# A fused attention and two-layer kernel: reciprocal root as one power operation on GpSimd, and another list scheduler's order

## The chip, the cores and the metric

The kernel runs on one core of a Trainium2 chip. The core has a matrix engine (TensorE, PE in the rows), whose weight loads are shown apart as PEld; VectorE (DVE), ScalarE (ACT) and GpSimd (POOL) for elementwise work; SyncE (SP), which here only issues transfers (DMA); and 16 DMA engines that move data between HBM and the on-chip memory. Each engine works off its own instructions in order; engines wait for each other through semaphores. The metric is the time of one execution in microseconds on the device; the median of three runs is quoted.

## What is computed

The reference has three parts, one after the other (cut to its core):

```python
# attention: q, k, v of 4 x 8 x 576 x 64
out_up    = np.repeat(sm_attn(mean4(q), mean4(k), mean4(v)), 4, axis=2)   # on means of 4 rows
out_local = softmax(where(|i - j| < 4, q @ k.T / 8, -1e9)) @ v            # a band of 7 keys
x = (out_up + out_local) as 2304 rows of 512
# first layer
h = x @ w_in                                       # 512 x 2048
x = (max(h, 0) + alpha * min(h, 0)) @ w_out        # 2048 x 512
# second layer
rms = np.sqrt(np.mean(x * x, axis=-1, keepdims=True) + 1e-06)
xn  = x / rms * rms_g
g   = xn @ w_gate                                  # 512 x 1536
return (g / (1 + exp(-g)) * (xn @ w_val)) @ w_out2 # 1536 x 512
```

The weights arrive as 64-bit floats.

## The kernel before

The 2304 rows are worked in six blocks of 384 (BW; half blocks of CW = 192), always with the rows along the free axis of a matmul and 128 features along the partitions. Each 32-bit product is made of three 16-bit matmuls, from a high and a low part of both operands (`split`, L373 and L374, makes the parts on ACT and DVE).

**Start.** Batch 0's attention needs q and k of each pair of heads transposed: `load` (L743) fetches each pair of heads in four transfers of 144 KB (two of q, two of k), PE transposes pieces of 96 rows (tps, L792), ACT copies three of them at a time to the tile T (L793, in all 16 such copies). Scores (lsps, L868 to L880, for the band; sps, L815, for the means), exponentials (L900, L825) and the sums over v follow. At the same time the weights of the first layer are made ready: a w_in tile of 768 KB is loaded (wr, L1091), decoded from 64-bit to 32-bit floats by two ACT instructions (L1110, L1113) and one on DVE (L1115), its size is measured on PE (sqps, L1131), and it is split.

**Stages.** `m1_first` runs the first layer for blocks 0 and half of 1, then `m1` and `m2` alternate over the blocks: `m1` (hps, L1371; acc, L1388) is the first layer, `m2` (gps, L1488; oacc, L1517) the second. In between stands `rms_tasks` for each of the six blocks: squares on ACT, column sums by matmuls with ones (ssps, L1309), in `ssum` the mean and its reciprocal root (the tile ry of 128x3 numbers, L1320 to L1330, eleven of its instructions on DVE the Newton iteration with its start value), in `bcast` three matmuls that spread ry over the partitions (rps, L1336), then the scaling (ra, L1345) and the split into x (L374). The attention of the other batches (prod, L478 and L526, partly on POOL; sd, L632) and the second layer's weights are cut into small tasks, which the slots of the stages call in the background.

**What sets the order.** The kernel is written out in program order first, and `issue_order` then reorders it: a list scheduler that gives each instruction a duration (`cost`), a delay to those that need its result (`waits`), and walks forward and backward over the graph in turn, 40 rounds, each with the end times of the last as priorities. The round with the earliest end of its own model is kept, and each engine's queue, the queue of SP included, is fixed in that order. Nothing of it is adjusted on the device: an instruction that waits holds all behind it on its engine. Eight transfers can be under way; the ninth issue waits until the first has landed.

Of the kernel before, what the change touches and what calls it, by code (L numbers as in the profile page):

```python
# [9 lines left out]
F32 = mybir.dt.float32  # L10
F16 = mybir.dt.float16
I32 = mybir.dt.int32
# [8 lines left out]
    return bass.AP(tensor=ap.tensor, offset=ap.offset + off, ap=[p] + [list(d) for d in dims])  # L21


def issue_order(tc, nc, groups, rounds=40):


    insts = [i for i in nc.cur_bb.bb.instructions if i.opcode != "TilePoolBoundary"]
# [22 lines left out]
    def psum(a):  # L50
        return "PSUM" in str(a.tensor.space)
# [34 lines left out]
    def cost(k, ins, outs):  # L86
        i, e = insts[k], eng[k]
        if not outs:
            return 60.0
        o, n = outs[0], free(outs[0])  # L90
        if e == "SP":
            return transfer(o, ins[0])[0]
        if e == "PE":
            if wide(ins[0]) == 2:
                return n / 2.4 + (2.5 if n > 128 else 50)
            return n * 2 / 2.4 + 4 if i.is_transpose else n * 4 / 2.4 + 100
        n = max([n] + [free(a) for a in ins[:1]])
        extra = len([a for a in ins[1:] if free(a) == 1 and n > 1])
        if e == "Activation":
            return (51 if psum(ins[0]) else 93) + n / 1.2 + 93 * (extra + len(outs) - 1)  # L100
        if e == "DVE":
            if i.opcode == "Reciprocal":
                return 89 + 6.25 * n
            fast = i.opcode in ("TensorScalarPtr", "TensorCopy") and not any(psum(a) for a in ins)
            fast = fast and len([a for a in ins if free(a) > 1]) < 2
            return 89 + n / (1.92 if fast else 0.96) + 60 * (extra > 0)
# [98 lines left out]
    def run(P, S, prio, fwd, d):  # L205
# [33 lines left out]
                        heapq.heappush(soon[eng[s]], (at[s], s))  # L239
        return end, seq, real  # L240

    prio, d, best = [float(-k) for k in count], dur, None
    for _ in range(rounds):
        end = run(succs, preds, prio, False, d)[0]
        end, seq, d = run(preds, succs, [-x for x in end], True, dur)
        prio = [-x for x in end]
        if best is None or max(end) < best[0]:
            best = max(end), seq
    info = mybir.DependencyInfo(mybir.DependencyClass.NoSync, mybir.DependencyReason.DATA)
    for q in best[1].values():  # L250
        for a, b in zip(q, q[1:]):
# [4 lines left out]
def kernel(  # L256
# [62 lines left out]
    ident = const.tile([128, 128], F32, name="ident")  # L319
    ones = const.tile([128, 1], F32, name="ones")  # L320
    nhalf = const.tile([128, 1], F32, name="nhalf")
    maskp = const.tile([128, 2, W, ND], F32, name="maskp")
    edge = const.tile([128, 3], F32, name="edge")
    pidx = edge[:, 2:3].bitcast(I32)
# [51 lines left out]
    def setup():  # L376
        nc.gpsimd.memset(ident, 1.0)
        nc.gpsimd.affine_select(
            out=ident, in_=ident, pattern=[[-1, 128]], compare_op=ALU.is_equal, fill=0.0, base=0, channel_multiplier=1
        )  # L380
        nc.vector.memset(ones, 1.0)
        nc.vector.memset(nhalf, -0.5 - 2.0 ** -20)
        nc.gpsimd.iota(pidx, pattern=[[0, 1]], base=0, channel_multiplier=1)
        nc.vector.tensor_scalar(out=edge[:, 0:1], in0=pidx, scalar1=HP, scalar2=NEG, op0=ALU.is_lt, op1=ALU.mult)
        nc.vector.tensor_scalar(out=edge[:, 1:2], in0=pidx, scalar1=(NC - 1) * HP, scalar2=NEG, op0=ALU.is_ge, op1=ALU.mult)
        nc.gpsimd.memset(maskp, 0.0)
        for t in range(W):
# [901 lines left out]
    def rms_tasks(m):  # L1289
# [23 lines left out]
        NT = BW // 128  # L1313

        def ssum():
            v_ = x1_p.tile([128, 3, NT], F32, tag="ry", name="ry")
            x, y, t_ = v_[:, 0], v_[:, 1], v_[:, 2]
            p = st["ps"][:, :, 0]
            if ne > 1:
                nc.vector.tensor_reduce(out=x, in_=st["ps"], axis=AX.X, op=ALU.add)  # L1320
                p = x
            nc.vector.tensor_scalar(out=x, in0=p, scalar1=1.0 / DM, scalar2=1e-6, op0=ALU.mult, op1=ALU.add)
            nc.vector.tensor_scalar(out=y.bitcast(I32), in0=x.bitcast(I32), scalar1=1, scalar2=None,
                                    op0=ALU.logical_shift_right)
# [421 lines left out]
```

## Time and profile before

| | |
|---|---|
| median of three runs | 969.99 us (968.99 to 970.92) |
| the profiled execution | 967.56 us |
| its span, from the first to the last instruction | 965.8 us |
| TensorE busy | 929.6 us, 96% |
| VectorE busy | 685.5 us, 71% |
| ScalarE busy | 481.7 us, 50% |
| GpSimd busy | 117.5 us, 12% |
| granted TensorE clock, mean | 0.991 of full speed |

The rows below come from one profiled execution. "Busy" is the share of time in which an engine has an instruction under way; a row of a group shows how often it stands (x), its busy time, the mean length of one, and the idle time just before it with what ended it. A row of the order of time may merge equal neighbours (x2). Lengths of matmuls contain their latency: the pace is read from a run of many.

### The profile page before, as it was taken

The numbers are of one execution on the slowest core, as the hardware profiler recorded it, in microseconds if no ns is written. First come the engines' busy times: TensorE is split into PE (matmuls) and PEld (weight loads), VectorE is DVE, ScalarE is ACT, GpSimd is POOL, SyncE is SP. The second block draws the span as 40 slices with busy tenths as digits, with TensorE's granted clock in tenths as the row PEclk, the third lists the DMA queues.
The fourth block names the chain that finished last, engine by engine and source line by source line (L and its number), as shares of the span: only waits on it lengthen the run. The fifth ranks groups of instructions, "written<-read, shape, count | busy, mean of one in ns | idle before, by whom it ended". The sixth has DMA issues, their size and how long they took to land.

```text
span 965.8 us, 16581 instructions
## 1 busy us (share of the span) xinstructions
PE 929.6 (96%) x6484; PEld 600.2 (62%) x6484; DVE 685.5 (71%) x1447; ACT 481.7 (50%) x1108; POOL 117.5 (12%) x96
## 2 busy tenths in 40 slices
PE   6978999999999999999999999999999999999998
PEld 4767777799655555565566655555556666555554
DVE  4789996998999978999987899963333442542333
ACT  5999889889864273233575322221322433321322
POOL 1101100201021103333102313210000000000000
PEclk9978999999999999999999999999999999999999
DMA  8886534574302142122122211000000000000000
GB/s 207 253 274 181 161 100 137 197 226 155 128 1 58 52 141 95 44 72 62 45 85 73 82 38 36 22 22 1 20 14 1 1 1 1 1 1 10 24 1 33
DMA packets 53712, 73.80 MB, mean 76 GB/s; under 512 B 22190, under 2 KB 35138, under 8 KB 53634
## 3 DMA queue, kind: packets, MB, share of 16 engines
q1 hardware_dynamic: 53634, 72.74, 24.9%
q8 instruction: 51, 0.84, 0.4%
q14 instruction: 27, 0.22, 0.1%
HBM read 68.01 MB, written 4.72 MB: 75 GB/s over the span
## 4 chain that ended last, share of the span: by engine, by line
PE 67%; DVE 13%; ACT 9%; issue 6%; DMA 5%; POOL 0%; SPq 0%; ACTq 0%; POOLq 0%
PE gps L1488 23%; PE hps L1371 12%; PE acc L1388 12%; PE oacc L1517 11%; DMA out_dram<-ob 4%; DVE prod L539 2%; DVE ls L489 1%; ACT wr L1110 1%; ACT dls L900 1%; DVE prod L526 1%; ACT wr L1113 1%; ACT wi L373 1%; DVE ghl L374 1%; DVE prod L478 1%; DVE hps L1377 1%
## 5 line engine op out<-in xcount | busy, mean ns | idle before, releaser
L1371 PE MATMUL hps<-xt,wi 128*128 128x192 f16 (+1 forms) x1536 | 357.0, 290 | 7.2 <-DVE g L374 3.8
L1488 PE MATMUL gps<-x,w 128*128 128x384 f16 x1728 | 339.0, 326 | 3.3 <-DVE th L1499 3.0
L1388 PE MATMUL acc<-ghl,wo 128*128 128x384 f16 (+1 forms) x960 | 253.8, 310 | 1.7 <-DVE ghl L374 0.6
L1488 PEld LDWEIGHTS <-w 128*128 128x128 f16 x1728 | 169.9, 99 | 118.4 <-issue 5.2
L1517 PE MATMUL oacc<-w,uhl 128*128 128x512 f16 x630 | 191.5, 379 | 2.3 <-ACT ob L1573 1.6
L1371 PEld LDWEIGHTS <-wi 128*128 128x128 f16 x1536 | 149.5, 100 | 59.4 <-issue 7.3
L1388 PEld LDWEIGHTS <-wo 128*128 128x128 f16 x1344 | 129.0, 98 | 61.7 <-issue 4.5
L1377 DVE SCALAR_TENSOR_TENSOR hps<-g,oma,hps 128x192 f32<-128x192 f32 (+1 forms) x128 | 66.0, 516 | 61.3 <-ACT g L1375 61.0
L1497 ACT ACTIVATE th<-gps,tsc 128x384 f32<-128x384 f32 x72 | 41.8, 580 | 132.3 <-PE gps L1488 131.8
L1517 PEld LDWEIGHTS <-uhl 128*128 128x128 f16 x630 | 61.6, 98 | 67.3 <-issue 2.4
L1499 DVE SCALAR_TENSOR_TENSOR th<-th,gps 128x384 f32<-128x384 f32 x72 | 39.6, 550 | 87.8 <-ACT th L1497 87.4
L1375 ACT ACTIVATE g<-hps 128x384 f32<-128x384 f32 x96 | 47.3, 493 | 84.1 <-PE hps L1371 83.5
L1508 ACT ACTIVATE uhl<-gps 128x384 f16<-128x384 f32 x72 | 41.7, 579 | 94.3 <-DVE gps L1502 85.5
L478 POOL TENSOR_TENSOR prod<-cq,ckv 128x896 f32<-128x896 f32 x24 | 54.8, 2284 | 191.6 <-DVE ls L489 50.6
L1388 PE MATMUL acc<-g,wo 128*128 128x384 f16 (+1 forms) x384 | 70.4, 286 | 0.0
L373 ACT ACTIVATE ghl<-hps,grp 128x384 f16<-128x384 f32 (+1 forms) x73 | 42.0, 576 | 51.2 <-DVE hps L1377 48.6
L1509 DVE TENSOR_TENSOR uhl<-gps,uhl 128x384 f16<-128x384 f32 x72 | 45.3, 629 | 28.1 <-ACT uhl L1508 27.8
L526 POOL TENSOR_TENSOR prod<-ls,ckv 128x896 f32<-128x896 f32 x24 | 43.6, 1816 | 163.3 <-DVE lo L539 70.6
L539 DVE TENSOR_TENSOR prod<-prod 128x384 f32<-128x384 f32 (+1 forms) x96 | 59.4, 630 | 4.3 <-POOL prod L526 4.3
L374 DVE SCALAR_TENSOR_TENSOR ghl<-hps,grp,ghl 128x384 f16<-128x384 f32 (+1 forms) x73 | 44.3, 607 | 23.9 <-ACT ghl L373 23.6
L489 DVE TENSOR_REDUCE ls<-prod 128x14 f32<-128x896 f32 x48 | 51.1, 1075 | 0.1
L1110 ACT ACTIVATE wr<-wr 128x768 f32<-128x768 f32 (+1 forms) x48 | 41.8, 877 | 6.2 <-DMA wr<-in_moe_w_out_dram 3.2
(242 smaller groups left out, 1138.9 us busy)
## 6 DMA issues: line engine op xcount, KB each, us to landing
wr<-in_moe_w_out_dram SPq DMA_DIRECT2D x18, 512.0 KB
wr<-in_moe_w_in_dram SPq DMA_DIRECT2D x10, 768.0 KB
wr<-in_moe_w_gate_dram SPq DMA_DIRECT2D x8, 768.0 KB
wr<-in_moe_w_val_dram SPq DMA_DIRECT2D x8, 768.0 KB
ckv<-in_k_dram SPq DMA_DIRECT2D x7, 768.0 KB
ckv<-in_v_dram SPq DMA_DIRECT2D x7, 768.0 KB
wr<-in_moe_w_out_dram SPq DMA_DIRECT2D x20, 256.0 KB
sd<-in_q_dram SPq DMA_DIRECT2D x24, 144.0 KB
```

Of the source, the lines that this page charges most:

```text
L373: nc.scalar.activation(out=hi, in_=src, func=AF.Copy, scale=s)
L374: nc.vector.scalar_tensor_tensor(out=lo, in0=src, scalar=s, in1=hi, op0=ALU.mult, op1=ALU.subtract)
L478: engs[i].tensor_tensor(out=pr, in0=view(st["q"][:, j, t:t + TP], [[D, TP], [0, ND], [1, D]]), in1=view(st["k"][:, j, t:t + TP], [[D, TP], ...
L489: nc.vector.tensor_reduce(out=st["s"][:, j, t:t + TP], in_=st.pop(("p", i)), axis=AX.X, op=ALU.add)
L526: engs[i].tensor_tensor(out=pr, in0=view(st["s"][:, j, t:t + TP], [[ND, TP], [1, ND], [0, D]]), in1=view(st["v"][:, j, t:t + TP], [[D, TP] ...
L539: add = lambda o, a, c: nc.vector.tensor_tensor(out=o, in0=a, in1=c, op=ALU.add)
L1110: nc.scalar.activation(out=hi.bitcast(F32), in_=hi.bitcast(F32), func=AF.Prelu, scale=2.0 ** -112, alpha=2.0 ** 32)
L1371: nc.tensor.matmul(ps[:, j], wi[:, f + j, a, kk * 128:(kk + 1) * 128], x[:, b_, kk, c0:c0 + n], start=(i == 0), stop=(i == 3 * KK - 1))
L1377: nc.vector.scalar_tensor_tensor(out=ps[:, j], in0=g[:, j], scalar=oma[:, f + j:f + j + 1], in1=ps[:, j], op0=ALU.mult, op1=ALU.add)
L1388: nc.tensor.matmul(acc[e], wo_f(f)[:, a, e * 128:(e + 1) * 128], hl[:, b_], start=(f == f0 and i == 0), stop=(f == f1 and i == 2))
L1488: nc.tensor.matmul(ps, w2_t[i0 + f // 3].rearrange("p a (k c) -> p a k c", k=KK)[:, a, kk, (f % 3) * 128:(f % 3 + 1) * 128], xh[:, b_, kk] ...
L1517: nc.tensor.matmul(acc[tt], t[:, a, tt * 128:(tt + 1) * 128], w[:, b_, f % 3], start=(f in first and i == 0), stop=(f in last and i == 2))
```

## The change

Three things change. `ssum` keeps the mean on DVE (L1320 and L1322) and replaces the eleven instructions of the Newton iteration by one on GpSimd: ry to the power -0.5, with a constant tile mhalf as exponent. In `issue_order` some durations of `cost` are other numbers (small matmuls, ScalarE with a stepped input, VectorE's fixed part and its reads from PSUM, 1200 ns for a GpSimd operation on up to four numbers). And the choice among the rounds changes: 100 rounds are run instead of 40, each candidate order within 8 us of the best so far is walked through by the new function `replay`, in which each queue is kept as it stands, under three sets of durations (as estimated; ScalarE 3% and transfers 10% slower; VectorE 3% slower and transfers 5% faster; each with another phase of the TensorE clock), and the smallest mean of the three ends is kept. Lines of the kernel proper stand 39 higher than before (L743 is L782, L1110 is L1149, L1322 is L1361), from `bcast` on 32 higher (L1336 is L1368).

```diff
-def issue_order(tc, nc, groups, rounds=40):
+def issue_order(tc, nc, groups, rounds=100):
...
             if wide(ins[0]) == 2:
-                return n / 2.4 + (2.5 if n > 128 else 50)
-            return n * 2 / 2.4 + 4 if i.is_transpose else n * 4 / 2.4 + 100
+                return max(25.0, n / 2.4 + 2.5)
+            return n * 2 / 2.4 + 3 if i.is_transpose else n * 4 / 2.4 + (128 if n < 64 else 8)
...
+        if n <= 4 and ins:
+            return 1200.0
...
-        if best is None or max(end) < best[0]:
-            best = max(end), seq
+        if best is None or max(end) < best[0] + 8000.0:
+            x = sum(replay(seq, *a) for a in trials) / len(trials)
+            if best is None or x < best[0]:
+                best = x, seq
...
+        nc.gpsimd.memset(mhalf, -0.5)
...
             nc.vector.tensor_scalar(out=x, in0=p, scalar1=1.0 / DM, scalar2=1e-6, op0=ALU.mult, op1=ALU.add)
-            nc.vector.tensor_scalar(out=y.bitcast(I32), in0=x.bitcast(I32), scalar1=1, scalar2=None,
-                                    op0=ALU.logical_shift_right)
-            nc.vector.tensor_scalar(out=y.bitcast(I32), in0=y.bitcast(I32), scalar1=-1.0, scalar2=float(0x5F3759DF),
-                                    op0=ALU.mult, op1=ALU.add)
-            for _ in range(3):
-                nc.vector.tensor_tensor(out=t_, in0=y, in1=y, op=ALU.mult)
-                nc.vector.scalar_tensor_tensor(out=t_, in0=t_, scalar=-0.5, in1=x, op0=ALU.mult, op1=ALU.mult)
-                nc.vector.scalar_tensor_tensor(out=y, in0=t_, scalar=1.5, in1=y, op0=ALU.add, op1=ALU.mult)
+            nc.gpsimd.tensor_tensor(out=y, in0=x, in1=mhalf.to_broadcast([128, NT]), op=ALU.pow)
```

The order changes nearly everywhere on the way, by a few places. Three places follow. The first is SP's queue at the start, from the fourth transfer on (wo holds the raw q and k, wr a raw weight tile). Before:

```order
L743 DMA wo<-in_k_dram 96x6x64
L743 DMA wo<-in_q_dram 96x6x64
L743 DMA wo<-in_k_dram 96x6x64
L743 DMA wo<-in_q_dram 96x6x64 x2
L743 DMA wo<-in_k_dram 96x6x64
L1650 DMA rows<-in_moe_alpha_dram 16x128
L1650 DMA rows<-in_moe_rms_g_dram 4x128
L743 DMA wo<-in_k_dram 96x6x64
L743 DMA wo<-in_q_dram 96x6x64
L1091 DMA wr<-in_moe_w_in_dram 128x2x768
```

and now:

```order
L782 DMA wo<-in_k_dram 96x6x64
L1130 DMA wr<-in_moe_w_in_dram 128x2x768
L782 DMA wo<-in_q_dram 96x6x64
L782 DMA wo<-in_k_dram 96x6x64
L782 DMA wo<-in_q_dram 96x6x64
L1130 DMA wr<-in_moe_w_in_dram 128x2x768
L782 DMA wo<-in_k_dram 96x6x64
L782 DMA wo<-in_q_dram 96x6x64
L782 DMA wo<-in_k_dram 96x6x64
L1682 DMA rows<-in_moe_alpha_dram 16x128
```

The first w_in tile moved from the fourteenth transfer to the fifth, ahead of the later head loads, and the second to the ninth. The second place is ACT's queue at the start (T is the copy of the transposes, wr the decode). Before:

```order
L793 ACT_TABLE_LOAD
L793 ACTIVATE T_183<-tps 128x3x96 x4
L793 ACTIVATE T_188<-tps 128x3x96 x3
L825 ACTIVATE dd,dsum<-sps,dm 72x144 x2
L793 ACTIVATE T_188<-tps 128x3x96
L825 ACTIVATE dd,dsum<-sps,dm 72x144 x2
L1110 ACTIVATE wr<-wr 128x768
L793 ACTIVATE T_198<-tps 128x3x96
L1113 ACTIVATE wr<-wr,nhalf 128x768
```

and now:

```order
L1149 ACT_TABLE_LOAD
L1149 ACTIVATE wr<-wr 128x768
L1152 ACTIVATE wr<-wr,nhalf 128x768
L832 ACTIVATE T_185<-tps 128x3x96 x4
L832 ACTIVATE T_190<-tps 128x3x96
L1149 ACTIVATE wr<-wr 128x768
L1152 ACTIVATE wr<-wr,nhalf 128x768
L832 ACTIVATE T_190<-tps 128x3x96 x3
L864 ACTIVATE dd,dsum<-sps,dm 72x144 x4
```

Two decodes moved ahead of the first eight T copies; one of them now stands first. The third is DVE around the reciprocal root of block 1 (th, gps and uhl belong to the second layer, w to the preparation of its weights, eb, tsc and inv to its scales). Before, from the mean on:

```order
L1322 TENSOR_SCALAR ry<-ssps 128x3
L1252 TENSOR_SCALAR tsc<-eb_117,rg_116 128x1
L1256 SCALAR_TENSOR_TENSOR inv_122<-eb_117 128x1
L1323 TENSOR_SCALAR ry<-ry 128x3
L1499 SCALAR_TENSOR_TENSOR th<-th,gps 128x384
L1258 TENSOR_SCALAR inv_122<-inv_122,rg_116 128x1
L1325 TENSOR_SCALAR ry<-ry 128x3
L1502 SCALAR_TENSOR_TENSOR gps<-th,gps 128x384
L1328 TENSOR_TENSOR ry<-ry 128x3
L1400 TENSOR_TENSOR inv_105<-sc 128x1
L374 SCALAR_TENSOR_TENSOR w_3809<-wc,sw_118,w_3809 128x1536
L1329 SCALAR_TENSOR_TENSOR ry<-ry 128x3
```

and now, around the mean, which is all of it that is left on DVE:

```order
L1541 TENSOR_TENSOR uhl<-gps,uhl 128x384
L1295 SCALAR_TENSOR_TENSOR inv_123<-eb_118 128x1
L1534 SCALAR_TENSOR_TENSOR gps<-th,gps 128x384
L412 SCALAR_TENSOR_TENSOR w_3801<-wc,sw_119,w_3801 128x1536
L1297 TENSOR_SCALAR inv_123<-inv_123,rg_117 128x1
L1361 TENSOR_SCALAR ry<-ssps 128x3
L528 TENSOR_REDUCE ls<-prod 128x14
L1541 TENSOR_TENSOR uhl<-gps,uhl 128x384
L517 TENSOR_TENSOR prod<-cq,ckv 128x896
L400 TENSOR_SCALAR s_115<-allps 128x1
```

and the place of the power operation in POOL's queue, which had only the products (prod) there:

```order
L949 TENSOR_TENSOR dls<-dls,dlsum 96x408 x10
L517 TENSOR_TENSOR prod<-cq,ckv 128x896 x3
L1362 TENSOR_TENSOR ry<-ry,mhalf 128x3
L565 TENSOR_TENSOR prod<-ls,ckv 128x896 x3
L517 TENSOR_TENSOR prod<-cq,ckv 128x896 x2
```

The eleven steps are gone from DVE, and the operation of block 0 stands behind three products on POOL, that of block 1 (the row after these) behind two more of the next group.

## Rows read from the trace of the kernel before

**Rows 1.** The page: busy time by engine; GB/s in 40 slices of 24 us.

```profile
PE 929.6 (96%) x6484; PEld 600.2 (62%) x6484; DVE 685.5 (71%) x1447; ACT 481.7 (50%) x1108; POOL 117.5 (12%) x96
...
GB/s 207 253 274 181 161 100 137 197 226 155 128 1 58 52 141 95 44 72 62 45 85 73 82 38 36 22 22 1 20 14 1 1 1 1 1 1 10 24 1 33
```

**Rows 2.** Stretch, length, busy PE, PEld, DVE, ACT, POOL; clock, DMA share, GB/s.

```profile
0.00:8.00 8.00, 1.80 (x10) 1.62 (x10) 1.06 (x9) 1.28 (x1) 2.05 (x26) 1.00 0.65 144
8.00:24.00 16.00, 13.67 (x83) 9.76 (x81) 9.37 (x31) 11.61 (x38) 1.14 (x1) 1.00 0.96 237
24.00:60.00 36.00, 32.23 (x263) 26.29 (x262) 25.42 (x70) 32.86 (x96) 3.73 (x3) 0.91 0.81 259
60.00:100.00 40.00, 32.24 (x340) 27.48 (x341) 37.41 (x86) 39.77 (x103) 4.26 (x8) 0.87 0.71 212
100.00:240.00 140.00, 137.58 (x1463) 117.11 (x1461) 123.88 (x304) 124.47 (x288) 16.73 (x13) 1.00 0.52 160
240.00:480.00 240.00, 233.48 (x1466) 139.11 (x1464) 223.77 (x444) 112.01 (x250) 54.44 (x26) 1.00 0.23 71
480.00:660.00 180.00, 179.36 (x1115) 106.23 (x1112) 149.94 (x298) 69.22 (x174) 35.12 (x20) 1.00 0.17 50
660.00:966.00 306.00, 299.28 (x1758) 172.57 (x1756) 114.62 (x210) 90.48 (x165) 0.00 (x0) 1.00 0.03 9
```

**Rows 3.** ScalarE in order of time: start, length, what; idle before it in brackets.

```profile
0.81 1.28 ACT L793 ACT_TABLE_LOAD   x1 [0.81 <-PEq L1730]
8.20 1.18 ACT L793 ACTIVATE T<-tps 128x288 f32<-128x288 f32 x2 [6.11 <-PE tps L792]
10.05 1.18 ACT L793 ACTIVATE T<-tps 128x288 f32<-128x288 f32 x2 [0.67 <-PE tps L792]
...
14.30 0.67 ACT L793 ACTIVATE T<-tps 128x288 f32<-128x288 f32 x1 [1.72 <-PE tps L792]
...
17.86 0.90 ACT L1110 ACTIVATE wr<-wr 128x768 f32<-128x768 f32 x1
...
19.11 0.96 ACT L1113 ACTIVATE wr<-wr,nhalf 128x768 int32<-128x768 uint32 x1
```

**Rows 4.** The chain of waits, in order of time: start, length, what.

```profile
3.64 3.35 DMA wo<-in_q_dram
...
112.34 0.99 PE hps L1371 x12
...
634.36 3.58 PE gps L1488 x22
...
638.31 1.51 PE oacc L1517 x7
```

**Rows 5.** The tile ry: one group of its steps, ns minimum/median/maximum.

```profile
L1328 DVE TENSOR_TENSOR ry<-ry x18: 146/156/166, 202.7 to 840.2; 128x3 f32<-128x3 f32 x18
```

**Rows 6.** Block 4, VectorE and then TensorE in order of time.

```profile
768.62 0.16 DVE L1322 TENSOR_SCALAR ry<-ssps 128x3 f32<-128x3 f32 x1 [1.39 <-PE ssps L1309]
...
775.92 0.38 PE L1336 MATMUL rps<-ident,ry 128*128 128x128 f32 x2
```

**Rows 7.** Groups of instructions on GpSimd: count, busy us, mean ns, idle before.

```profile
L478 POOL TENSOR_TENSOR prod<-cq,ckv 128x896 f32<-128x896 f32 x24 | 54.8, 2284 | 191.6 <-DVE ls L489 50.6 <-PE qkps L644 45.2 <-DVE dm L663 39.2
...
L910 POOL TENSOR_TENSOR dls<-dls,dlsum 96x408 f32<-96x408 f32 x12 | 11.4, 967 | 116.7 <-DVE dlsum L907 115.0 <-ACT wi L373 1.7
...
L972 POOL MEMSET T<- 128x3 f32 x4 | 0.3, 103 | 4.8 <-PE lsps L880 4.8
```

**Rows 8.** Groups of instructions on VectorE.

```profile
L632 DVE TENSOR_TENSOR sd<-sd 72x512 f32<-72x512 f32 x36 | 25.1, 697 | 4.5 <-ACT dd L619 4.5
...
L374 DVE SCALAR_TENSOR_TENSOR w<-wc,sw,w 128x1536 f16<-128x1536 f32 x12 | 23.2, 1935 | 1.5 <-ACT w L373 1.5
...
L663 DVE TENSOR_REDUCE dm<-sps 72x2 f32<-72x288 f32 x24 | 9.9, 449 | 3.4 <-PE sps L657 3.2
```

**Rows 9.** Whom TensorE waited for from 100 to 660 us: us, times, longest.

```profile
PE gps L1488 <- DVE th L1499: 3.0, 4, 1.0
```

More of the change, by code (lines that the diff above doesn't have):

```diff
@@ L99, in cost @@
         if e == "Activation":
-            return (51 if psum(ins[0]) else 93) + n / 1.2 + 93 * (extra + len(outs) - 1)
+            odd = ins and not psum(ins[0]) and list(ins[0].ap)[-1][0] != 1
+            return ((51 if psum(ins[0]) else 93) + n / (1.09 if odd else 1.2) + 93 * (extra + len(outs) - 1)
+                    + 20 * (wide(o) == 2))
         if e == "DVE":
@@ L105, in cost @@
             fast = fast and len([a for a in ins if free(a) > 1]) < 2
-            return 89 + n / (1.92 if fast else 0.96) + 60 * (extra > 0)
+            if ins and psum(ins[0]) and list(ins[0].ap)[-1][0] > 2:
+                return 69 + n / 0.58
+            return max(150, 69 + n / (1.92 if fast else 0.96) + 60 * (extra > 0))
+        if n <= 4 and ins:
+            return 1200.0
         if i.opcode == "TensorTensor":
@@ L240, in run, with replay @@
         return end, seq, real
+    def replay(seq, factors, phase):
+        by = dict(zip(("Activation", "DVE", "SP"), factors))
+        pos, clock = dict.fromkeys(engines, 0), {e: 2100.0 if e == "Activation" else 600.0 for e in engines}
+        left, at = [len(p) for p in preds], [0.0] * len(insts)
+        port, last = 0.0, 0.0
+        win, done, slow = 0, 0, True
+        for _ in count:
+            t, e = min((max(clock[e], at[seq[e][pos[e]]]), e) for e in engines
+                       if pos[e] < len(seq[e]) and not left[seq[e][pos[e]]])
+            k = seq[e][pos[e]]
+            pos[e] += 1
+            f = by.get(e, 1.0)
+            x = f * dur[k]
+            if e == "PE":
+                while t + phase >= (win + 1) * WIN:
+                    slow, win, done = done < BUSY, win + 1, 0
+                done += work[k]
+                x = (2 * x - 2.5 if slow else x) + fixed[k]
+            if shared[k]:
+                x += max(0.0, port - t)
+                port = t + x
+            last = max(last, t + x)
+            clock[e] = t + (x if held[k] is None else f * held[k])
+            for s in succs[k]:
+                left[s] -= 1
+                at[s] = max(at[s], t + x + lag(k, s))
+        return last
+    trials = (((1.0, 1.0, 1.0), 0.0), ((1.03, 1.0, 1.1), 1700.0), ((1.0, 1.03, 0.95), 800.0))
     prio, d, best = [float(-k) for k in count], dur, None
@@ L321 @@
     nhalf = const.tile([128, 1], F32, name="nhalf")
+    mhalf = const.tile([128, 1], F32, name="mhalf")
     maskp = const.tile([128, 2, W, ND], F32, name="maskp")
@@ L1315, in ssum @@
         def ssum():
-            v_ = x1_p.tile([128, 3, NT], F32, tag="ry", name="ry")
-            x, y, t_ = v_[:, 0], v_[:, 1], v_[:, 2]
+            v_ = x1_p.tile([128, 2, NT], F32, tag="ry", name="ry")
+            x, y = v_[:, 0], v_[:, 1]
             p = st["ps"][:, :, 0]
```

## The prediction

> **What bounds the kernel now.** I read the page first: TensorE (PE) is busy 929.6 of the span's 965.8 us [rows 1], so at most 36 us can be won without taking matmuls away, and the change takes none away. Then the windows [rows 2] say where those 36 us lie: subtract PE's busy time from each stretch's length. The first 100 us lose 6.2 + 2.3 + 3.8 + 7.8 = 20.1 us, the next 560 us (100 to 660) only 2.4 + 6.5 + 0.6 = 9.6 us, the end 6.6 us. In the first 100 us ScalarE (ACT) is the engine that works through: 32.9 of 36 us in the stretch from 24 us, 39.8 of 40 in the one from 60 us; from 240 to 480 us it is VectorE (DVE), 223.8 of 240. So the start is an ACT matter, the middle leaves PE little to wait for, and what counts at the start is when ACT gets going. [Rows 3] show that: ACT loads its table, then stands idle until 8.20 us for the first transpose (tps), and is idle again in small pieces, 0.67 us twice, 1.72 and 0.60 us (of the two 0.67 one row stands, the 0.60 is before the next tps copy at 15.57). Up to the eighth T copy at 16.73 us that is 0.81 + 6.11 + 0.67 + 0.67 + 1.72 + 0.60 = 10.6 us of idle ACT. The first decode of a w_in tile (L1110, L1113) stands only at 17.86 us. The chain of waits [rows 4] names the cause of the late start: the fifth head load, issued at 3.64 us, landed 3.35 us later, at 6.99 us.
>
> **The change part by part.**
>
> *The power operation.* It removes from each of the six row blocks eleven VectorE instructions on 128x3 elements, 66 in all, at 0.156 us [rows 5]: 10.3 us of DVE. It adds one GpSimd (POOL) operation per block. In the program before, PE has 7.3 us of matmuls in block 4 between the sum's arrival at 768.62 and the broadcast rps at 775.92 [rows 6], so the eleven steps are covered, and their removal is worth nothing to PE by itself. The cover of the new chain is counted from the new PE order: between the last ssps and the first rps stand 77 matmuls of 192 columns in block 0 (0.082 us each by 0.99 us for 12 [rows 4]: 6.3 us), 25 of 384 and 12 of 512 columns in block 1 (0.163 and 0.216 us: 4.1 + 2.6 = 6.7 us); blocks 2, 3 and 5 have over 11 us, and block 4's order is unchanged. Ahead of the pow stand in block 0 a weight split on DVE (1.94 us [rows 8]), three short steps (0.7 us) and a POOL product (2.28 us [rows 7]); half of the two long ones on average makes 2.8 us, all of them 4.9. In block 1 likewise 2.5, or 4.6. The pow itself is not in the trace. Its lower bound is the 128x3 memset, 0.10 us, its upper one the longest two-input operation on POOL, 2.28 us; I take 0.97, the shortest two-input row there (96x408), because the fixed part must be most of it [rows 7]. Then the chain takes 3.8 and 3.5 us under covers of 6.3 and 6.7: **no cost**. At 2.28 us with everything in front it would cost 4.9 + 2.28 - 6.3 = 0.9 and 4.6 + 2.28 - 6.7 = 0.2, together 1.1 us.
>
> *VectorE's freed time.* Four of the six blocks lie where DVE is full. But PE's waits there for a DVE result are small, the largest 3.0 us in all [rows 9], and the new order puts other work into the freed slots (ahead of the tenth th step (L1499) DVE has no less work than before). I take **0**, and up to 3.0 us gain for the range.
>
> *The order at the start.* SyncE (SP) now issues the first w_in tile (768 KB) as fifth transfer, where a 144 KB head load stood, and a second as ninth. ACT decodes the first before any transpose copy, the second after five of them. Both engines are in order: the copies wait behind the decode, and the decode waits for its tile. At a rate r (kB per us, the same as GB/s), the first tile lands at 6.99 + 639/r (624 KB more than the load that landed at 6.99), the second after 442 kB of head loads and its own 786 kB: 6.99 + 1867/r. ACT needs 1.28 us for the table, 0.90 + 0.96 for a decode, 5 x 0.59 for the copies [rows 3], 6.1 us in all, before the second decode. Its idle time up to there is thus 6.99 + 1867/r - 6.1, against the 10.6 us of before: a gain of 9.7 - 1867/r. With the 237 GB/s of 8 to 24 us [rows 2], where head loads and tiles are mixed, it is **1.8 us**. With the 144 of the first 8 us it is a loss of 3.3 us; with the third slice's 274 GB/s [rows 1] ACT itself is last, and the gain is 2.5 us. I take 237 because the queue is filled then; the 144 is a mean over a stretch that begins before the first transfer. After that the same work stands ahead of the eighth g copy on ACT, to within 0.3 us: 0.
>
> *PE's extra work.* Ahead of the 193rd hps matmul PE has 16 more small matmuls of the next batch's attention, at 0.082 us 1.3 us of work done earlier. PE is idle for a fifth of 60 to 100 us [rows 2], so that much of it would have been free anyhow: **1.0 us** gain, between 0 and 1.3.
>
> *The rest of the order* (100 to 660 us) moves hundreds of instructions by a few places; PE can gain there no more than the 9.6 us that it idles. From 685 us on PE's order is the same row by row. I take 0.
>
> Sum: 1.8 + 1.0 = 2.8 us. The profiled execution took 967.56 us, 1.76 more than its span; that gives 964.8. The median of the runs, 969.99, is 2.43 above it, so the forecast is **967.2 us**.
>
> **The rivals.**
>
> *The gain is given back by 100 us.* Ahead of the fifteenth hps step (L1377) DVE has six instructions more than before, the longest of 0.70 us, two of 0.45 [rows 8]; at 0.45 on average 2.7 us, and DVE is busy 37.4 of 40 us there [rows 2]. If DVE is what PE waits for, 2.8 - 2.7 = 0.1 us remains: 969.9. For it speak the full DVE and PE's many small waits; against it that ACT is fuller still.
>
> *The start is held behind the w_in tiles* (the slower side). The first transposes of PE wait for the load right behind the first tile. If the tiles move at the first stretch's 144 GB/s, ACT loses 3.3 us and PE does its extra work no earlier: 973.3. It decides below r = 1867/9.7 = 193; to be slower by over 0.2% without the extra work, 1.9 us, below 161. For it speaks that head loads of 256 B pieces fill the queue first; against it the first slice's mean of 207, idle beginning included [rows 1].
>
> *The pow holds the broadcast.* PE is in order, and hps or gps matmuls stand behind rps. It decides from a pow of 3.5 us in block 0 and 4.2 us in block 1. At 4.6 us, twice the longest row, it costs 1.1 + 0.4, so 968.7; at 6.8 us it costs 3.3 + 2.6, so 973.1. Against it: no POOL row of this size is over 2.3 us on average [rows 7]. The Trainium skill (GPSIMD Engine Reference, 2.1 Instruction dispatch) says that the first call of a freshly loaded GpSimd kernel pays about 6 us (5.95) with no instruction to show for it. Were the pow such a call, it would be late once, in block 0, by 5.95 - 3.5 = 2.5 us on this page's figure, and the time would be 969.7. No row here shows it yet.
>
> That the change doesn't do what it says is excluded: the new order has the six pow operations and none of the Newton steps.
>
> **How the numbers follow.** About 0.2%, 1.9 us, is what a measurement of this kernel can tell from no change: faster is below 968.05, slower above 971.93. The forecast has 0.49, with its own range of 964 to 968; giving back 0.28, of which 0.03 beyond 971.93; the held start 0.15, all slower; the long pow 0.08, half within, half slower. Faster 0.49; within 0.28 - 0.03 + 0.04 = 0.29; slower 0.15 + 0.03 + 0.04 = 0.22. The range goes from 962.5 (1.3 + 2.5 + 3.0 us gained, and 0.7 more in the middle) to 972.5; it leaves out most of the held start and little else.
>
> **What would show it.** In the profile after: ACT's first decode between 9 and 10.5 us and the T copies from 11.5 us on; idle ACT up to the eighth copy near 8.8 instead of 10.6 us; PE's idle time in the first 100 us down from 20.1 to some 17 us, with the rest of the stretches as they were; pow rows of about 1 us, and no wait of PE for rps. Wrong would be: the first decode later than 12 us, PE's waits for a DVE result longer in 60 to 100 us, or a PE gap before rps near 200 or 280 us. If PE's idle time falls between 240 and 480 us instead, the freed DVE was worth what I set at nothing.

## The result, and the profile after

The change made the kernel slower: 975.6 to 980.6 us in five runs against 967.9 to 970.9 us in six runs of before on the same chip; the ratio is **1.0091, 95% interval 1.0069 to 1.0113**. (A sixth run of after, 5343 us, and below a sixth run of g2, 2415 us, are far outside all others and are left out.) The forecast was 967.2 us. The profiled run of after took 975.61 us, 1.9 us more than its span, against 967.56 us of before: 8.05 us to be found.

The page of after, busy time by engine [rows 1]:

```profile
span 973.7 us, 16531 instructions
...
PE 931.5 (96%) x6484; PEld 603.6 (62%) x6484; DVE 680.3 (70%) x1381; ACT 482.1 (50%) x1108; POOL 122.6 (13%) x103
```

TensorE runs the same 6484 matmuls and is busy 1.9 us longer; its idle time went from 36.2 to 42.2 us. VectorE lost 66 instructions and only 5 us: the 10.3 us of small steps are gone, others together grew by some 5 us. The windows of after, with the columns of [rows 2] (stretch, length, busy PE, PEld, DVE, ACT, POOL, clock, DMA share, GB/s):

```profile
0.00:8.00 8.00, 0.93 (x4) 0.71 (x4) 1.07 (x9) 1.28 (x1) 2.08 (x27) 1.00 0.65 179
8.00:24.00 16.00, 12.05 (x67) 8.64 (x68) 9.31 (x23) 12.85 (x32) 1.14 (x1) 1.00 1.16 261
24.00:60.00 36.00, 33.66 (x250) 27.81 (x249) 22.32 (x67) 28.64 (x95) 4.46 (x3) 1.00 0.75 218
60.00:100.00 40.00, 29.39 (x316) 25.03 (x314) 36.08 (x86) 39.15 (x88) 4.19 (x8) 0.87 0.74 218
100.00:240.00 140.00, 134.68 (x1424) 113.11 (x1425) 124.26 (x288) 126.14 (x303) 20.55 (x14) 1.00 0.53 167
240.00:480.00 240.00, 235.56 (x1518) 145.27 (x1515) 220.67 (x430) 107.94 (x230) 51.15 (x26) 0.99 0.21 68
480.00:660.00 180.00, 177.90 (x1111) 105.84 (x1110) 153.05 (x290) 74.23 (x196) 37.32 (x22) 1.00 0.18 52
```

Length less busy PE, against [rows 2]: the first 100 us idle 24.0 instead of 20.1 us, 100 to 240 us 5.3 instead of 2.4, 240 to 480 us 4.4 instead of 6.5, 480 to 660 us 2.1 instead of 0.6. How far TensorE is behind can be read off too, as both kernels have the same matmuls to do and the clock after 100 us is near full in both: take the busy time up to a point from the total of the page. At 100 us 855.5 us are left in after and 849.7 before, so after is 5.8 us behind; at 240 us it is 8.7, at 480 us 6.6, at 660 us 8.1. Most of the loss is there by 100 us. And read the ACT column: up to 24 us ScalarE has done 14.1 us of work, 1.2 more than before. From 24 to 60 us it then does 28.6 instead of 32.9 us. By 100 us it is 3.6 us behind the kernel before.

ScalarE's start, as in [rows 3]:

```profile
8.99 0.88 ACT L1149 ACTIVATE wr<-wr 128x768 f32<-128x768 f32 x1 [6.91 <-DMA wr<-in_moe_w_in_dram]
9.77 1.00 ACT L1152 ACTIVATE wr<-wr,nhalf 128x768 int32<-128x768 uint32 x1
10.84 1.22 ACT L832 ACTIVATE T<-tps 128x288 f32<-128x288 f32 x2
...
14.58 0.68 ACT L832 ACTIVATE T<-tps 128x288 f32<-128x288 f32 x1 [0.67 <-PE tps L831]
15.05 0.91 ACT L1149 ACTIVATE wr<-wr 128x768 f32<-128x768 f32 x1
...
18.67 0.67 ACT L832 ACTIVATE T<-tps 128x288 f32<-128x288 f32 x1 [0.32 <-PE tps L831]
```

ScalarE can start on the first tile at 8.99 us, the copies start at 10.84, the second decode at 15.05, without a wait for its tile; the idle pieces up to the eighth copy add to 9.7 us (10.6 before). TensorE pays for it: its first transpose now waits for the head load behind the tile, until 9.77 us instead of 7.13 (before, then after):

```profile
7.13 1.19 PE L792 MATMUL tps<-ident,wo 96*128 96x96 f32 x6 [3.64 <-DMA wo<-in_q_dram]
...
9.77 1.19 PE L831 MATMUL tps<-ident,wo 96*128 96x96 f32 x6 [6.27 <-DMA wo<-in_q_dram]
```

The chain of waits has that load as 5.33 us from issue to landing, 3.35 in [rows 4]:

```profile
4.30 5.33 DMA wo<-in_q_dram
```

Whom ScalarE waited for from 24 to 60 us in after (us, times, longest), and in before:

```profile
ACT aT L883 <- PE atps L882: 5.1, 4, 2.1
ACT laT L965 <- PE ltps L963: 0.9, 1, 0.9
```

```profile
ACT aT L844 <- PE atps L843: 1.4, 1, 1.4
```

Its aT copies stand at the head of its queue while TensorE, which is full in that stretch (33.7 of 36 us), still has other matmuls ahead of the transposes (atps) that they read. From 60 to 100 us ScalarE is full, and TensorE waits for weights (wc) that were decoded late. In after, then before:

```profile
PE sqps L1170 <- DVE wc L1158: 6.7, 4, 2.0
...
PE sqps L1131 <- DVE wc L1119: 2.1, 2, 1.7
```

The power operation, in the tile ry as in [rows 5]:

```profile
L1368 PE MATMUL rps<-ident,ry x36: 272/275/376, 210.4 to 858.1; 128*128 128x128 f32 x36
L1362 POOL TENSOR_TENSOR ry<-ry,mhalf x6: 849/850/1512, 206.8 to 846.4; 128x3 f32<-128x3 f32 x6
...
  POOL prod L565: 19.7, 1
```

It takes 0.85 us at the median, and no wait of TensorE for rps is in the trace (in block 0 the sum is there at 204.2 us, the operation ends at 208.34, rps follows at 210.38, so 2.0 us were to spare). The 19.7 us that the view puts down to a GpSimd product behind it began when the operation had ended, so they are not its cost. From 100 to 660 us TensorE's waits for th are down from the 3.0 us of [rows 9] to 0.6, but others have come up:

```profile
PE acc L1420 <- ACT ghl L411: 2.2, 2, 2.0
...
PE acc L1420 <- DVE x L1502: 1.5, 1, 1.5
...
PE gps L1520 <- DVE th L1531: 0.6, 2, 0.4
```

### The profile page after: what moved, and what is told of

Its sections match the earlier page's. It is cut to its first block, busy times and chain, and to the rows that moved or that the text cites. A ratio compares the mean times of both kernels' runs of the same rounds, so it can differ in the third digit from the quotient of the medians.

```text
span 973.7 us, 16531 instructions
## 1 busy us (share of the span) xinstructions
PE 931.5 (96%) x6484; PEld 603.6 (62%) x6484; DVE 680.3 (70%) x1381; ACT 482.1 (50%) x1108; POOL 122.6 (13%) x103
## 4 chain that ended last, share of the span: by engine, by line
PE 71%; DVE 12%; ACT 8%; DMA 5%; issue 3%; POOL 1%; SPq 1%; ACTq 0%; DVEq 0%; POOLq 0%
PE gps L1520 21%; PE acc L1420 16%; PE hps L1403 15%; PE oacc L1549 10%; DMA out_dram<-ob 3%; DVE prod L578 1%; DVE ls L528 1%; ACT dls L939 1%; ACT wr L1149 1%; DVE prod L517 1%; ACT wr L1152 1%; PE tps L831 1%; DMA wr<-in_moe_w_val_dram 1%; PE sps L696 1%; DVE prod L565 1%
## 5 line engine op out<-in xcount | busy, mean ns | idle before, releaser
L1403 PE MATMUL hps<-xt,wi 128*128 128x192 f16 (+1 forms) x1536 | 350.1, 291 | 3.1 <-DVE g L412 2.1
L1520 PE MATMUL gps<-x,w 128*128 128x384 f16 x1728 | 350.8, 326 | 1.4 <-DVE uhl L1541 0.8
L1420 PE MATMUL acc<-ghl,wo 128*128 128x384 f16 (+1 forms) x960 | 246.5, 311 | 4.2 <-ACT ghl L411 2.2
L1549 PE MATMUL oacc<-w,uhl 128*128 128x512 f16 x630 | 201.2, 379 | 1.9 <-ACT ob L1605 1.9
L1420 PE MATMUL acc<-g,wo 128*128 128x384 f16 (+1 forms) x384 | 74.4, 286 | 0.0
L578 DVE TENSOR_TENSOR prod<-prod 128x384 f32<-128x384 f32 (+1 forms) x96 | 53.6, 569 | 1.4 <-POOL prod L565 1.2
L1149 ACT ACTIVATE wr<-wr 128x768 f32<-128x768 f32 (+1 forms) x48 | 41.8, 878 | 9.3 <-DMA wr<-in_moe_w_in_dram 6.9
```

The lines of the kernel that those rows point to most:

```text
L578: add = lambda o, a, c: nc.vector.tensor_tensor(out=o, in0=a, in1=c, op=ALU.add)
L1149: nc.scalar.activation(out=hi.bitcast(F32), in_=hi.bitcast(F32), func=AF.Prelu, scale=2.0 ** -112, alpha=2.0 ** 32)
L1403: nc.tensor.matmul(ps[:, j], wi[:, f + j, a, kk * 128:(kk + 1) * 128], x[:, b_, kk, c0:c0 + n], start=(i == 0), stop=(i == 3 * KK - 1))
L1420: nc.tensor.matmul(acc[e], wo_f(f)[:, a, e * 128:(e + 1) * 128], hl[:, b_], start=(f == f0 and i == 0), stop=(f == f1 and i == 2))
L1520: nc.tensor.matmul(ps, w2_t[i0 + f // 3].rearrange("p a (k c) -> p a k c", k=KK)[:, a, kk, (f % 3) * 128:(f % 3 + 1) * 128], xh[:, b_, kk] ...
L1549: nc.tensor.matmul(acc[tt], t[:, a, tt * 128:(tt + 1) * 128], w[:, b_, f % 3], start=(f in first and i == 0), stop=(f in last and i == 2))
```

## The experiments

The planner's order is not one that an edit leaves alone: each new number moves hundreds of instructions. So most runs here fix the order. In these kernels the end of issue_order takes a list in place of a plan,

```diff
-    for q in best[1].values():
+    for e, length in LENGTHS.items():
+        ...
         for a, b in zip(q, q[1:]):
             tc.add_manual_dep(insts[b], insts[a].name, info, reason="issue order")
```

and the list is put together from the orders of before and after: an early part cut off by time, together with whatever its instructions need first. Each kernel ran five to twelve times beside before (medians 969.4 to 970.2 us); the bracket behind a ratio is its 95% interval. Theory A: the new order costs the time. Rival B: the power operation does.

### Operation and order apart

**e1: the old order, with the power operation.**

```diff
-            for _ in range(3):
-                nc.vector.tensor_tensor(out=t_, in0=y, in1=y, op=ALU.mult)
...
+            nc.gpsimd.tensor_tensor(out=y, in0=x, in1=mhalf.to_broadcast([128, NT]), op=ALU.pow)
```

> The order of before on every engine, fixed instruction by instruction; only the six chains of eleven VectorE steps give way to the six power operations, each placed on GpSimd where the order of before has room for it. Theory A (the new order costs the time, the power operation nothing): no change from before, 968.8 us, within 1 us either way. Rival B (the power operation costs the time, by holding the broadcast or GpSimd's products): slower by most of the 9 us, 975 to 979 us. If VectorE's freed 10.3 us are worth anything by themselves, the time falls below 967 us.

Measured: 969.19 us, ratio 1.0002 (0.9991 to 1.0014). B falls: the operation costs nothing and VectorE's freed time is worth nothing, to within 0.14%.

**e2: the new order, with the Newton steps** (the diff of e1 reversed, eleven steps in one piece).

> The order of after on every engine, fixed; the power operation is taken out and the eleven VectorE steps stand in one piece behind the sum of each row block. Theory A: as slow as after, 975 to 980 us (the chains may add up to 1 us where VectorE is full). Rival B: back at the time of before, 968 to 970 us.

Measured: 983.52 us (976.3 to 985.5), 1.0136 (1.0111 to 1.0162). Taking the operation out brings nothing back. The extra over after was not taken apart: besides the lump of eleven steps, the first tile came only at 10.56 us here.

**e3 and e4: new start with old rest, old start with new rest**, cut at about 100 us.

> With the power operation: of the instructions that before issues in about its first 100 us, the order of after; of all others, the order of before. By the windows of the two traces the first 100 us of after lose 3.9 us more idle TensorE and about 1.9 us of matmuls at the lower clock. Theory A1 (both parts of the order cost): 972 to 975 us. Theory A2 (all of it comes from the start): 976 to 979 us. Theory A3 (the start costs nothing in the end, since the lost work is made up later): 968 to 970 us.

> The reverse, with the power operation: the first 100 us in the order of before, all others in the order of after. Theory A1: 971 to 974 us, so that the extra of this one and of the new start with the old rest add to some 8 to 10 us. Theory A2: 968 to 970 us. Theory A3: 976 to 979 us.

Measured: e3 976.62 us (975 to 984), 1.0095 (1.0067 to 1.0123); e4 971.79 us, 1.0034 (1.0019 to 1.0049). The start is the larger part: e3 lies where A2 had it, but e4 where A1 had it, so the rest costs too. Their sum, 1.29%, is above after's 0.91% by about as much as the intervals allow, and e3's profiled run, its slowest, has waits for transfers from 24 to 60 us that after hardly has (2.0 us of ScalarE for a tile, 3.3 us of TensorE for v), so the loss can't be split exactly. In e4, window 100 to 240 us first, then the same of e1:

```profile
100.00:240.00 140.00, 133.65 (x1388) 112.80 (x1388) 122.42 (x280) 122.88 (x282) 21.81 (x14) 0.99 0.52 164
```

```profile
100.00:240.00 140.00, 137.63 (x1454) 116.59 (x1454) 121.63 (x288) 122.49 (x283) 17.10 (x14) 1.00 0.52 157
```

TensorE idles 6.4 instead of 2.4 us there; from 240 to 480 us e4 wins 2.0 us back, from 480 to 660 us it loses 1.6. Of the 4.0 us one wait has a name, 1.5 us near 230 us for the step that adds up the first layer's output (x, L1502), which the old order had in time; the other new ones are under 1 us each.

### The start taken apart

**f1 and f2: the old order, with the two tiles early.** SyncE's list, and in f1 ScalarE's too (f2 is the first half alone):

```diff
 L782 DMA wo<-in_k_dram
+L1130 DMA wr<-in_moe_w_in_dram
 L782 DMA wo<-in_q_dram
...
+L1149 ACTIVATE wr<-wr 128x768
+L1152 ACTIVATE wr<-wr,nhalf 128x768
 L832 ACTIVATE T<-tps 128x3x96
```

> The order of before with the power operation (969.2 us with before at 969.6), and one thing of the new order: SyncE issues the first two w_in tiles as fifth and ninth transfer, and ScalarE decodes the first ahead of all T copies and the second behind five. All else stands in the old order. Theory S (this move is the loss of the new start): 974 to 979 us, with some us between one run and the next, as the first tile lands at 9 or at 12 us. Rival T (what is ordered otherwise from 24 to 100 us is the loss): 968 to 971 us. What the prediction counted, a gain of 1.8 us: 967 us.

> Only SyncE's half of that move: the two w_in tiles go out fifth and ninth, but ScalarE decodes them where the old order has them, behind the T copies. If the loss is the head loads that come later for TensorE's first transposes (2.6 us later in after), 971.5 to 973 us; if it is ScalarE waiting for the tile in front of its T copies, 968.5 to 970 us; if theory T is right, 968.5 to 970 us too.

Measured: f1 971.62 us (969.4 to 977.4), 1.0024 (1.0007 to 1.0041); f2 973.12 us (969.6 to 975.7), 1.0033 (1.0018 to 1.0048). So the move alone costs 2 to 3 us where I had counted a gain of 1.8; f1 lies between the two theories, f2 just above its range. In f2 only SyncE's queue differs from e1, ScalarE waits for no tile and it is no better: so the loads that now come later do it, the first head load among them (TensorE's first transpose at 9.78 us in f2, 10.99 in f1). But ScalarE's long waits for atps from 24 to 60 us don't come from there. In f1, then f2, they are small:

```profile
ACT aT L883 <- PE atps L882: 0.3, 1, 0.3
...
ACT aT L883 <- PE atps L882: 1.3, 1, 1.3
```

The rest of the new start's loss lies elsewhere.

**f6: after, with the old first 24 us.** **d3: the old order, ScalarE late** by nine activations that nothing reads:

```diff
+    for _ in range(9):
+        nc.scalar.activation(out=late, in_=mhalf.to_broadcast([128, 256]), func=AF.Copy, scale=1.0)
```

> The order of after, but what before issues in about the first 24 us (217 of 8827 instructions, all head loads, the first T copies and decodes) stands in the old order. Theory S: the loss of the start is gone, 970 to 973 us, as with the old order over the first 100 us (971.8 us). Rival T: 975 to 979 us, as after.

> The old order with the power operation, and nine activations of 128x256 elements that nothing reads, some 0.30 us each, behind ScalarE's second T copy: ScalarE comes 2.7 us later to all that follows. If time lost on ScalarE at the start comes back one for one at the end, as the prediction took it, 971.9 us; if its idle pieces or later slack take it in, 969 to 970 us; if it grows on the way (TensorE at the lower clock for longer), over 973 us.

Measured: f6 978.75 us, 1.0092 (1.0070 to 1.0113): no repair. One reason shows at the seam: the old start issues the third tile late, the new continuation decodes it early, ahead of the softmax steps dd, and TensorE waits 4.5 us for these. So f6 doesn't prove that the first 24 us are harmless; it shows that these two pieces of plans don't fit each other. Its waits for atps are 5.5 us though its first loads are on time. d3: 971.99 us, 1.0020 (1.0006 to 1.0033): the nine steps took 0.415 us each, 3.7 us, and cost 0.18% over e1, 1.7 us, about half; with both intervals that is anything from 0 to 3.5 us.

### From 24 to 60 us

**h3: only 24 to 60 us in the new order**, cut as above.

> With the power operation: the old order up to about 24 us, the new order for what before issues from 24 to about 60 us (some 400 instructions), the old order for all that follows. In after ScalarE waits 5.1 us there for the transposes that its aT copies read (1.4 us before), and from 60 to 100 us, where ScalarE is full, TensorE then waits 6.7 us in four places for wc (2.1 us before). Theory U (what ScalarE stands idle from 24 to 60 us is missing when TensorE needs it, and comes back at the end): the aT waits are there, and 973 to 976 us. Rival V (the order of 60 to 100 us itself makes the wc waits): 968 to 970.5 us.

Measured: 977.97 us, 1.0085 (1.0070 to 1.0100). The waits for atps are there, 5.5 us, with the old first 24 us ahead of them:

```profile
ACT aT L883 <- PE atps L882: 5.5, 6, 2.1
```

They thus belong to the new order from 24 to 60 us. The loss is large, but with f6's seam in it: one decode waits 2.2 us for its tile and TensorE 6.4 us for the softmax steps dd, which the new order alone doesn't have. **i1** puts eleven idle activations (the diff of d3) into the old order instead; **i2** moves four decode steps of h3 ahead of the waits for atps:

```diff
+L1149 ACTIVATE wr<-wr 128x768
 L883 ACTIVATE aT<-atps
+L1152 ACTIVATE wr<-wr,nhalf 128x768
 L883 ACTIVATE aT<-atps
...
+L1149 ACTIVATE wr<-wr 128x768
+L1152 ACTIVATE wr<-wr,nhalf 128x768
 L883 ACTIVATE aT<-atps
```

> The old order with the power operation (969.2 us), and nothing else but eleven activations of 128x256 that nothing reads, 0.43 us each, 4.7 us in all, on ScalarE at three places from 45 to 53 us: about the time that ScalarE stands idle there in the new order. Theory U (ScalarE's lost time from 24 to 60 us is by itself the cause): 973 to 977 us. If it needs more than that (tiles, slots, the order of TensorE): under 972 us.

> The old order with the new one from 24 to 60 us (978.0 us), but four decode steps that stood behind ScalarE's waits for the transposes (0.8 to 1.0 us each, 3.4 us in all) stand ahead of these waits, where their tiles have landed. Theory U: 973 to 976 us, with the aT waits down from 5.5 us to some 2 us. If ScalarE's waits are a symptom of something else that is late: 977 to 980 us.

Measured: i1 971.87 us, 1.0026 (1.0012 to 1.0040): 4.6 us taken from ScalarE cost 0.24% over e1, 2.3 us (0.6 to 4.1 by both intervals). i2 978.29 us (974 to 984), 1.0087 (1.0060 to 1.0114): nothing regained, though ScalarE's waits for atps fell from 5.5 to 3.0 us. ScalarE only went on to wait elsewhere, as the windows 0 to 100 us of h3 and of i2 show (ACT is the fourth busy time):

```profile
0.00:100.00 100.00, 74.17 (x584) 60.26 (x584) 64.85 (x174) 77.54 (x207) 11.50 (x35) 0.93 0.75 213
```

```profile
0.00:100.00 100.00, 73.65 (x587) 59.66 (x587) 65.05 (x174) 78.21 (x208) 11.61 (x37) 0.95 0.76 214
```

So theory U holds only in part. Lost time of ScalarE alone cost about half of itself, with a wide margin (d3, i1), and i1 is below the range of U; that i2 regains nothing fits waits for atps that are a symptom. What does go together over all kernels with the old rest is ScalarE's work done by 100 us and the end. Useful ACT work by 100 us (idle activations taken off) and time, both of the profiled run, a single one that can lie some us off the median (e3's by 7.7 us; and d3 loses 4.5 us here where the ratios of all runs say 1.7):

| kernel | ACT by 100 us | us | missing against e1 | lost against e1 |
|---|---|---|---|---|
| e1 | 86.9 | 967.8 | 0 | 0 |
| f1 | 83.9 | 972.7 | 3.0 | 4.8 |
| f2 | 83.1 | 970.5 | 3.8 | 2.6 |
| d3 | 82.8 | 972.4 | 4.1 | 4.5 |
| i1 | 82.7 | 970.6 | 4.2 | 2.8 |
| i2 | 78.2 | 977.1 | 8.6 | 9.2 |
| h3 | 77.5 | 980.1 | 9.3 | 12.2 |
| e3 | 75.7 | 984.3 | 11.2 | 16.5 |

With the new rest it is e4 86.8 (971.0), after 81.9 (975.6), f6 80.0 (977.4). After is 4.9 us behind e4 in ACT work and 4.65 us in time. The row of e1 and that of after:

```profile
0.00:100.00 100.00, 78.42 (x692) 64.19 (x693) 74.69 (x197) 86.85 (x240) 11.07 (x39) 0.91 0.81 229
```

```profile
0.00:100.00 100.00, 76.02 (x632) 62.20 (x632) 68.78 (x184) 81.92 (x215) 11.87 (x39) 0.95 0.80 222
```

This is a measure of how far the start has come, not shown to be the cause: TensorE's matmuls done by 100 us fall in the same way (692 in e1, 656 to 661 in f1, f2, d3 and i1, 570 to 587 in i2, h3 and e3). And it holds only under one rest: of the plans of the next part, g1 has 87.2 us of ACT work by 100 us and takes 972.4 us, b1 84.3 us and 965.7 us.

### Which part of the planner

Four kernels with the power operation, planned anew: **g1** the old planner, **g2** new costs with the old choice, **g3** old costs with the new choice, and g3's idea taken apart: **c1** has of the new costs only those for TensorE, **c2** all but those.

```diff
             if wide(ins[0]) == 2:
-                return max(25.0, n / 2.4 + 2.5)
-            return n * 2 / 2.4 + 3 if i.is_transpose else n * 4 / 2.4 + (128 if n < 64 else 8)
+                return n / 2.4 + (2.5 if n > 128 else 50)
+            return n * 2 / 2.4 + 4 if i.is_transpose else n * 4 / 2.4 + 100
```

(c2 against after; in g3 all of cost() is the old one.)

> The power operation planned anew by the planner of before (its costs, 40 rounds, the shortest plan kept). The plan has the w_in tiles late, the first as sixteenth transfer, and ScalarE's decode behind the T copies. If the new cost numbers are what spoils the start, 967 to 971 us. If any new plan falls some us to one side or the other by chance, anything from 966 to 978 us.

> After with the choice of before: the new cost numbers, but 40 rounds and the shortest plan kept, no replays. Its plan has the w_in tiles early, as sixth and tenth transfer, like after. If the cost numbers spoil the start: 973 to 980 us, with TensorE's waits for wc from 60 to 100 us at some 7 us. If the choice by replays does it: 967 to 971 us.

> After with the cost numbers of before: 100 rounds and the choice by replays under three models. Its plan has the w_in tiles late, as before. If the cost numbers spoil the start: 967 to 971 us. If the choice by replays does it: 973 to 980 us.

> The faster plan (old costs, choice by replays: 965.6 us) with the three new cost lines for TensorE alone. Its plan has the first w_in tiles as sixth and tenth transfer. If TensorE's numbers make the bad start: 973 to 980 us. If they are harmless: 964 to 969 us.

> After with the old cost lines for TensorE, all else new. Its plan has the w_in tiles as thirteenth and eighteenth transfer. If TensorE's numbers make the bad start: 964 to 970 us. If those of ScalarE, VectorE or GpSimd do: 973 to 980 us.

| kernel | TensorE's cost lines | other cost lines | choice | w_in tiles | us | ratio |
|---|---|---|---|---|---|---|
| g1 | old | old | old | late | 974.4 | 1.0043 (1.0027 to 1.0060) |
| g2 | new | new | old | early | 979.1 | 1.0095 (1.0078 to 1.0112) |
| after | new | new | new | early | 975.6 to 980.6 | 1.0091 (1.0069 to 1.0113) |
| c1 | new | old | new | early | 971.1 (967 to 977) | 1.0015 (0.9992 to 1.0037) |
| c2 | old | new | new | late | 966.9 | **0.9962** (0.9946 to 0.9977) |
| g3 | old | old | new | late | 965.6 | **0.9954** (0.9935 to 0.9973) |

Give after its old TensorE lines back, and it is faster than before (c2). With the new lines the tiles come to the front in all three plans; but with them alone (c1) no loss is clear of the noise, and g1 and n1 below lose without them. One plan of each kind can't tell the part of the numbers from that of chance. An early tile isn't the whole of it either: c1 and g2 both have it as sixth transfer, with TensorE's first transpose at 7.25 and 7.69 us, and lie 0.8% apart. The old planner with the operation is no way out either (g1): its plan happens to be 0.4% slower, which I had not expected.

**n1** is before with the new choice alone, **b1** is g3 with the operation priced at 1200 instead of 153 ns:

```diff
+        if n <= 4 and ins:
+            return 1200.0
```

> Before with the new choice alone: 100 rounds and replays under three models; VectorE's Newton steps and the old cost numbers stay. If the 4 us that the old costs with the new choice win (965.6 us) come from the choice, and the power operation is worth nothing: 965 to 968 us. If they need VectorE's freed time: 968 to 971 us.

> The old cost numbers with the new choice and the power operation, and of the new cost numbers only the one for that operation (1200 instead of 153 ns; the trace shows 850). If only TensorE's cost lines do harm, this is as fast as the same kernel without that price: 964 to 968 us. If plans fall several us apart by chance whatever the numbers: up to 974 us.

Measured: n1 971.58 us, 1.0022 (1.0011 to 1.0032); b1 966.72 us, **0.9968** (0.9957 to 0.9980). n1 lies above both its ranges, b1 in the first of its own. Three different plans with the operation, the old TensorE lines and the new choice (g3, b1, c2) beat before by 0.3 to 0.5%. Without the operation the new choice won nothing here. Since e1 shows the operation to be worth nothing in a fixed order, it may help only by what room it gives a plan, or n1's plan is an unlucky one; one plan each can't tell. Where g3 wins, its windows against e1's:

```profile
100.00:240.00 140.00, 139.43 (x1486) 118.65 (x1484) 123.67 (x291) 124.98 (x286) 18.46 (x14) 1.00 0.53 160
240.00:480.00 240.00, 234.33 (x1473) 140.01 (x1472) 224.40 (x440) 114.43 (x257) 54.84 (x26) 1.00 0.23 71
```

```profile
240.00:480.00 240.00, 233.93 (x1473) 139.70 (x1471) 222.75 (x436) 112.61 (x250) 55.66 (x27) 1.00 0.23 72
```

TensorE idles 0.6 instead of 2.4 us from 100 to 240 us (e1's row stands above) and 5.7 instead of 6.1 in the next stretch. g3 is the version to keep: 0.46% faster than before, where after is 0.91% slower.

## Why the prediction was wrong, step by step

- **The power operation, no cost: right, its size partly by luck.** It took 0.85 us against the 0.97 taken, and e1 is at 1.0002. The chain in block 0 was 4.2 us, against the 3.8 taken, under 6.2 us of other matmuls: the mechanism held. But that the fixed part is most of the 0.97 us does not come out of the rows named for it: 0.97 us for 408 elements and 2.28 for 896 are nearly in proportion, so that 0.85 lies so near is luck; the bounds would have carried the conclusion alone. The Trainium skill's price for a first call (GPSIMD Engine Reference, 2.1 Instruction dispatch; about 6 us) doesn't appear: the first one of e1 began 0.1 us after its sum and took 0.87 us. GpSimd had run other two-input operations before, so it may not be such a call.
- **VectorE's freed time, 0: right** in a fixed order, by the same run.
- **The order at the start, +1.8 us: the step that failed.** It took ScalarE's idle time up to the eighth copy for the whole account of the start. That idle time fell by 0.9 us, half of the forecast, and ScalarE did get 1.2 us more done by 24 us. (The first decode came at 8.99 us, by the formula 9.7. The second came at 15.05, by the formula 14.9, but by luck: it began when ScalarE was free and waited for no tile.) Two things were left out of the sum. The tile holds up the loads behind it, the head load of TensorE's first transposes by 2.6 us; f1 and f2 put the move at a loss of 2.3 and 3.2 us. And the new order from 24 to 60 us was set at nothing, though ScalarE does 28.6 us of work there instead of 32.9: its waits for atps come with that order (5.5 us in h3 and f6, whose first loads are on time; 0.3 and 1.3 us in f1 and f2, whose first loads are late). That ScalarE's time comes back one for one at the end isn't borne out either: d3 and i1 together lost 4.0 us for 8.3 us of ScalarE.
- **TensorE's extra work, +1.0 us: not there.** Work done earlier is worth something only if the next wait isn't later by as much; TensorE's idle time from 60 to 100 us grew from 7.8 to 10.6 us. The prediction's own sign of being wrong stands there, longer waits for a VectorE result: 6.7 instead of 2.1 us for wc.
- **The rest of the order, 0: mis-sized.** It costs 0.34% or 3.3 us in e4; in after itself TensorE falls back by 2.3 us from 100 to 660 us. I bounded the gain there, 9.6 us of idle TensorE, and gave a loss no bound. Hundreds of moved instructions can lose as well as gain.
- **The rivals.** The held start was the right place and sign, but not the mechanism as I priced it: it was to begin where the tiles move below 193 KB per us, and from 8 to 24 us 261 were moved. That its 973.3 us is close to f1 and f2 (971.6 and 973.1) is luck. No rival had the rest of the order as a loss, so the range ended at 972.5.
- **Open:** f1 and e4 make 0.58 of the 0.91%, if they add. The remaining 3.2 us arise, by that sum, from the order of 24 to 100 us; h3 and f6 show that the order there is dear, but with a seam of their own, and i2 shows that it isn't only the four waits that one sees. What in that order costs the time is not shown.

## What to carry to other kernels

When a planner's numbers change together with an operation, fix the order first and measure the operation in it: here that took one run, and a second one with the roles exchanged, and showed that the loss was order. A moved order has to be given a loss as well as a gain: ask for each transfer pulled forward which load it now stands ahead of, and whether the engine that you relieve then waits for the one that you delayed. And other prices for single instructions give other plans, not by themselves better ones: here they fell from 0.5% faster to 1% slower than before. Time several plans before believing one.

## What the runs showed of the hardware

- **One transfer, four landings.** SyncE issued the first 768 KB tile at 3.62 or 3.63 us in all of these kernels, as fifth of the same first eight transfers; ScalarE could start on it at 8.99 us in after, 10.00 in f1, 10.56 in e2 and 11.89 in e3:

```profile
11.89 0.88 ACT L1149 ACTIVATE wr<-wr 128x768 f32<-128x768 f32 x1 [9.82 <-DMA wr<-in_moe_w_in_dram]
```

The times of f1, e3 and e2, which begin with the tile, scatter over 8.1, 9.4 and 9.2 us, those of g3, b1 and c2, which begin with the small loads, over 3.2, 2.8 and 2.0 us. That the tile does it isn't shown: g2 has it early and scatters over 3.4 us, i2 has it late and scatters over 9.5, and before itself over 8.8 in 23 runs.

- **The power operation is not always 0.85 us.** In after's block 0 it took 1.51 us, in e1's block 3 1.63 us. The traces of the 17 kernels that have it agree: whenever it took over 1 us, VectorE had a step with two operands in SBUF under way as it began, and it ended 0.71 to 0.73 us after that step (in after's block 0 wc<-wr, in e1's block 3 prod). Beside a step with one input (block 1 below) or with one operand in PSUM it took 0.85 to 0.87 us, and so it did in blocks 4 and 5. This looks like the operation waiting for the step that it meets; it was not tried apart.

```profile
206.67 0.94 DVE L1154 SCALAR_TENSOR_TENSOR wc<-wr 128x768 int32<-128x768 int32 x1
206.83 1.51 POOL L1362 TENSOR_TENSOR ry<-ry,mhalf 128x3 f32<-128x3 f32 x1 [3.95 <-DVE ry L1361]
...
281.69 1.07 DVE L528 TENSOR_REDUCE ls<-prod 128x14 f32<-128x896 f32 x1
281.85 0.86 POOL L1362 TENSOR_TENSOR ry<-ry,mhalf 128x3 f32<-128x3 f32 x1 [2.48 <-DVE ry L1361]
...
846.41 0.85 POOL L1362 TENSOR_TENSOR ry<-ry,mhalf 128x3 f32<-128x3 f32 x1 [68.94 <-DVE ry L1361]
```

- **A 128x256 activation of one broadcast column** took 0.415 us at the median in both kernels, where I had put 0.30 and 0.43; nine in a row took 4.00 us from the first start to the last end.
